# Sparse attention and a feed-forward layer on one core: new planned durations, a new order of loads and a new searched order

## The chip, the cores and the metric

One core of one Trainium2 chip runs the whole program. The metric is device time in microseconds (us); 0.5% of it is 1.2 us.

## What is computed

The reference, cut to what matters: a block-sorted attention, whose output is the input of a two-layer feed-forward part with a leaky rectifier. All inputs and the output are 32-bit floats.

```python
# q, k, v: (4, 8, 768, 64); sort_net: (4, 8, 8, 8); w_in: (512, 2048); w_out: (2048, 512)
P = sort_net
for _ in range(5):
    P = P - max(P, -1); P = exp(P)
    P = P / (sum(P, -1) + 1e-9)
    P = P / (sum(P, -2) + 1e-9)
k_sorted = einsum('bhij,bhjcd->bhicd', P, k_b)     # k, v in 8 blocks of 96 rows
v_sorted = einsum('bhij,bhjcd->bhicd', P, v_b)
scores = q_b @ k_sb.T / 8                          # block by block: 96 x 96
attn = softmax(scores)
x = (attn @ v_sb) as (3072, 512)
h = x @ w_in
g = maximum(h, 0) + alpha * minimum(h, 0)
out = g @ w_out
```

## The kernel before

**Units.** There are 4 batches of 8 blocks, 32 in all, called by number (block 8 is the first of batch 1). A block is 96 tokens with all 8 heads.

**Start (batch 0).** GpSimd issues the loads of q, k (two halves) and v (two halves), line 425 to 452, which convert to 16 bits on their way; the weights follow on the same queue (w_in in 8 pieces, L910, w_out in 2, L915), then k, q and v of batch 1 (KS, QN, VST). Meanwhile VectorE (DVE) and ScalarE (ACT) normalise the 8x8 sorting matrices in five rounds (`sinkhorn`, L518 to 543, result Pb), spread them over the partitions (L552 to 572, result BDK), and TensorE turns q (`prep_q`, L620), sorts and turns k (`prep_k`, L620, 6 units) and sorts v (`prep_v`, L688, 8 units). Before `prep_v`, v is laid out anew (`conv_v`, L677, 4 copies, each on GpSimd or DVE as the planner has it). Results go from PSUM to SBUF by copies on ACT or DVE (L402: QTz, KT, VS).

**Attention (`attention`, L709 on).** For a block: scores (L734), their maximum (L740, DVE). In batch 0 TensorE then computes the scores again with the maximum subtracted (L755, L746), ACT takes the exponential (L778, Es), the output matmul follows (L789), DVE divides (L796, L799, xq), TensorE turns xq (L814) and ACT or DVE copies it into xT. From block 8 on ("far") ACT takes eight exponentials (L767, Esb), a DMA transpose turns them (L772, ET<-Esb), the output matmul follows, and a second DMA transpose (L807) turns xq into xT. The transposes of q for batches 1 to 3 are on the same SP queue (L440, QTz<-QN), as are the output stores (L889).

**Feed-forward part.** `ffn1` (L836): xT by w_in, four matmuls for one of 16 feature tiles over 192 tokens (the first two chunks) or 384; ACT (L846) and DVE (L849) make the rectifier and write hT. Two PSUM banks (psH) take turns, and psYP helps in the first chunk. `ffn2` (L875): hT by w_out, 16 matmuls for 128 tokens in four parts, a copy to outstg (L402), a store (L889).

**What sets the order.** Everything is handed to a planner written into the kernel (`_Graph`). `add` records an operation with its engines, its reads and writes, a planned duration and a priority. `schedule` plays the operations through at build time: each engine takes, of those that are ready by its plan, the one with the lowest priority number, and `span` says when an operation frees its engine and when its result is there. So planned durations decide in which order each engine's instructions stand, and nothing else; on the chip each engine runs its list and waits on semaphores. The string ORDER holds a small number for each operation that is added to its priority; it comes from a search over orders. `span` has rules of its own for DMAs (from GpSimd `loads[0]`, from SP `loads[1]`), for a change of TensorE's tile shape (TILE_NS, `tiles`), and for TensorE's instruction fetch (FETCH, FETCH_NS: a fetch after each 256 instructions, not before 6000 ns after the last one until 58000 ns, 2500 ns after that). Loads of batch 3 wait for the transposes of certain blocks (`paced`).

**Fillers.** `fill` looks for gaps in TensorE's plan ahead of the first output matmul, the first `ffn1` and the first `ffn2`, and puts matmuls without use there (`warm`, L1012, 512 columns), as many as fit into 0.9 of the gap, at 430 ns each up to 6000 ns and 216 ns after.

Of the kernel before, what the change touches and what calls it, by code (L numbers as in the profile page):

```python
# [7 lines left out]
AP = bass.AP  # L8
# [26 lines left out]
FETCH = 256  # L35
FETCH_NS = 6000
FETCH0 = (70, -9000.0, 193)
ORDER = (
    "_o_y1piW010D0f8Q00pym3wBRMstCzMKKZTSWWPAYr3BQscQfaFSqtbihE2YztS9gxhSp8uPJt__IJUtnWBvhzp4dnkehSpmNaJ1Da4EURIcaIMJmV6YT2W0"
    "R2zacnQ3rYyOxuyrG0TzHEr76U6LPQ0G0bPVrYEg70s9y-GwRFyxgyubTIwFhnEwgk4UL2xqZL003Y1QOiPa4msA7MKM3WNS4qSW00UqVFW1prXPpn5Z2d00"  # L40
    "2K2R1g000k6q8e00oz004XHo00ACBuEiAm003zSQv2vFVW7zEcGDW6e-VtiC00T60000F526294EBR9-94Bn00BkDP2_iI7thc34B15Y72ux009rNJitN07q"
    "9iBK3g2JFy4014UDEw6Jvg2VSo3v007UXO0_05Pj0NCMKe3j9gMM3752bt0dvpOd33VpQT3N2l4N5l4YMY5-3o0B0K1YGQD5IC0U3d1K00W-000v1G08001F"
    "6w00S22I5X0pD-0I00Iy3900EkIzrP3QB_0J3qahMuFS3g004E5K002qF00b1a00cRht323q00tauA9DjK8r3Ssp4B132gPe5hWp6b3GFV5i2X0K2x2a565H"
    "1h6bh22C1pAU11gEId2S6S7T002DOzMWE3XiDhjgFZ681W00003223WZ1H1h0s3p5NSD2a0Ate00Jx1g319V0KpQ0t00Je1254303v1K3V007Z00gj1o891h"
    "1Cvr6d1r8rFiDVKxyhQu00CwFcYY8_DSVT9_Ky-ms7160G1v1QJi2sM6II8AEJHC6BH3G43l2A00ou1W4u6ElGGo00Cs01L4LdZp864tJfV900002TKe6fut"
    "7sHlLs1x2u6rNs4m001Y5-8krxRv19ZxZC002zb61uBIKYpBQgWGDPb8Dx00WfB60W40001PYE3z0024A1FY0-aS009m008r0js0Zxzkvuly5i0F00p9lx23"
    "0006AMNu3t00v4qj0xbV0yKwPM00q4-dNpviC2WDGj0U01580000CG6r5H000hSJ1WpN0300SkZF00f2Ha6909AOx95xds-61Ydk8uBPBojGApGCCCHbaN1T"
    "B9dS1P2C2C00QXg300GrBY0yPO0P0N7m4UxxP-FGtd3xeMXAWFQ-00al4hPS3j1k1lIY006ifn00NXPT1h752Y000000000KnHm_kD40Cr0z7n005eI8b5WO"
    "Jv1ZZbUw006B000hqBAT0000790A0023003A7R00000l0q3AWvDUWWsTgd4eyPVNtseSiZCmQgH3F-8O00qkFU00002e0O1M00Vd0Aqa4T-400Y44xEF00Dj"
    "5lth00D1iwFqNUcW9giS9C00O-Q3ck9xCPGAFnCEAQE21JDG7g2B00BE00MNv9oX1RK3Cd00fuE9H7k_bNGW3U7G0HCv00DF04006b7G0Y3g00003rEB000R"  # L50
    "590X00Hc6l8SDF9J5S009P5Shx00EEG00h3r003p6TCB004s1N007UFr009-ex005UOUxI4nGfF7SD5N007w110k2c3700790I00R73L002m0000U20000L5"
    "6T00Ey5W41MVeiML116aF1UbodhgGbq7f-5tJX3K6A8z02b3KF0r4GBZ1nGH3x0000BT2041Op4lBbCvBG0M01BcF100Ad78QO132V0BB-2100004Z07GT0e"
    "0n2h0P0Ud88V0S000y0S00003k0FAi00iI0PiTGL0Q1q0m00ms1a0000Bq005R7J2MCaCb00EW040061N41a1Y2A8P9I3F6FR55o3v001c9LLt1GepUi05Hj"
    "KE2d6m45XL29EvkvNn4AauGk002_411W6Q9m004N-6CH0m00004IUk00BG98Np00EmEA6d1Pki-U00Hg9G0Q2-E_4sKVBU0NCEVaQe0SkaChNC008k3O0000"
    "162tB36S009q7x1lEo140W1N27005rWW9B525tS4cl1YWd2i0Gb_6q4K170f5dBPSf1sh5001hMZiP01bhJDGv5-EXBdFX2PWh0K5r1BTs00FzCk69wsAg00"
    "0w3S00H-d200g9977681KDCRpB00Ot1t0L1z0000xM9E009Q2I00FyJhiT4D7MQgCk1f1GO40000000WlU1H14JLbP003yZL1B8e1D08uh3v00qdhy1F0I00"
    "0Pb-Vt2vluPj0HD12B4R2yC23-5G5U4m00Ne3EOI6x0n943N2j22002eAlA4005830006MAJ00DJ4s00O39F094K4_0R9VEM21091r00StK5004kFS1xaIL_"
    "00pyc53O2a001sZAhh000O0000ZCWk1v0B0z000P000Y000000Fqb-"
# [35 lines left out]
class _Graph:  # L94
# [67 lines left out]
    def schedule(self):  # L162
# [17 lines left out]
        loads = [0.0, 0.0, 0, *FETCH0]  # L180
# [5 lines left out]
        while done < len(ops):  # L186
# [9 lines left out]
            at, e, op = best  # L196
# [23 lines left out]
    def fill(self, make, spans):  # L220

        out, last = [], 0.0
        for op in self.order["pe"]:
            for lo, hi, deps, bank in spans:
                begin = max([last, lo] + [self.ops[d].end + 300 for d in deps])
                unit = 430 if begin < 6000 else 216
                m = int((op.start - begin) * 0.9 / unit)
                if op.start <= hi and m > 0:
                    x = _Op("pe", lambda e, m=m, bank=bank: make(e, m, bank), 0, 0.0, None, len(self.ops))
                    x.start, x.end = begin, begin + m * unit  # L230
                    x.deps.update(deps)
                    self.ops.append(x)
                    out.append(x)
# [77 lines left out]
def bass_sinkhorn_attn__then__act_prelu_kernel(  # L311
# [92 lines left out]
    def t_either(n, mode=1):  # L404
# [3 lines left out]
    G.add(SYNC, lambda e: e.dma_start(P32[:, :], AP(sort_net.tensor, 0, [[64, 32], [1, 64]])), 1990,  # L408
          w=["P"], prio=-100, dma=(dma_sem("sn"), 0))
    G.add(SYNC, lambda e: e.dma_start(alphaR[:, :], AP(moe_alpha.tensor, 0, [[128, 16], [1, 128]])),  # L410
          300, w=["alphaR"], prio=-99, dma=(dma_sem("al"), 0))
# [14 lines left out]
    def load_q(b, prio):  # L426
# [4 lines left out]
        for h in range(H):  # L431
# [4 lines left out]
                dma=(d_qn[h], 2000 * (b == 3)))  # L436

    def turn_q(b, t, prio):
# [6 lines left out]
            prio=prio, dma=(d_qt[t], 0))  # L445

    def load_kv(t, src, name, sem, g, b, prio):
        n = (2, 1, 1, 4)[b]
        for x in range(n):
# [4 lines left out]
                prio=prio + x / 100, dma=(sem[b + x + (b > 0)], 700 * (b == 3 and name == "KS")))  # L454
# [66 lines left out]
    def sinkhorn():  # L521
        pr = -85

        def dv(fn, r, w):
            G.add(DVE, fn, 210, r=r, w=w, prio=pr)
# [100 lines left out]
    def prep_q(u, prio, bank):  # L626
        t, off, row, keys = bank
        G.add(PE, pairs(KZ, 0, u, identb, 0, 128, bank, 6144), 372, r=[("QS", 0), "identb"], w=keys, prio=prio, tiles=(1, 1), mms=16)
# [4 lines left out]
    def conv_k(b, u, prio):  # L633
        n = b % 2
        for hp in range(2):
            o = AP(KZ, hp * 64 * 6144 + 16 * u * 128 + hp * 64, [[6144, 64], [128, 16], [1, 64]])
            i = AP(KS[n], hp * 64 * 3072 + 16 * u * 64, [[3072, 64], [64, 16], [1, 64]])
            G.add(POOL, lambda e, o=o, i=i: copy(e, o, i), 1600,
                  r=[("KS", n, x) for x in range(4)] + [("KZ0", hp)], w=[("KZ", u, hp)], prio=prio)

    def prep_k(b, u, prio, bank=BANK_P):
# [11 lines left out]
        else:  # L653
            G.add(PE, pairs(KS[n], n, u, BDK, b * 128, 512, bank), 372, r=[("KS", n, x) for x in ((u // 3,) if b == 0 else range(4))] + [("BDK", b)], w=keys,
                  prio=prio, tiles=(1, 1), mms=16)
# [9 lines left out]
    def conv_v(b, c, prio):  # L665
        keys = [("VD", 2 * c), ("VD", 2 * c + 1)]
        if b > 1:
            for th in range(2):
                oz = AP(VD32, th * 64 * 4096 + 8 * c * 128 + th * 64, [[4096, 64], [128, 8], [1, 48]])
                iz = AP(VST32[b % 2], th * 64 * 1536 + 8 * c, [[1536, 64], [1, 8], [32, 48]])  # L670
                G.add(POOL, lambda e, oz=oz, iz=iz: e.tensor_copy(oz, iz), 900,  # L671
# [5 lines left out]
        G.add(("dve", "pool"), lambda e: e.tensor_copy(o, i), {"dve": 560, "pool": 1000},  # L677
              r=[("VST", b % 2, x) for x in range(4)], w=keys + [("VDh", 2 * c), ("VDh", 2 * c + 1)], prio=prio)

    def prep_v(b, u, prio, bank=BANK_P):  # L680
# [21 lines left out]
        else:  # L702
            G.add(PE, f, 374, r=[("VD", u), ("VDh", u), "VD0", ("BDK", b)], w=keys, prio=prio, tiles=(1, 1), mms=16)
# [9 lines left out]
    def attention(g, prio):  # L713
# [49 lines left out]
        if far:  # L763
            def ex(e):
# [9 lines left out]
                5000 if g < 18 else 3100, r=[("Esb", me)], w=[("ET", me), ("turned", g)], prio=prio, dma=(d_e[me], 0))  # L774
# [31 lines left out]
        if far:  # L806
            G.add(SYNC, lambda e: e.dma_start_transpose(o2, AP(xq[me], 0, [[512, 96], [1, 512]])),  # L807
                  4400 if g < 18 else 2600, r=[("xq", me)], w=[("xT", g % 16), ("turnx", g)], prio=prio, dma=(d_x[me], 0))
# [49 lines left out]
    def ffn2(t, prios):  # L858
# [11 lines left out]
        for x, (bank, key) in enumerate(banks):  # L870
            for part in range(4):
# [11 lines left out]
                if len(ffn_ops) == 1:  # L883
# [8 lines left out]
                  dma=(d_o[ob + x], 0))  # L892
# [115 lines left out]
    def warm(e, m, bank):  # L1008
        t, off, row, keys = bank
        inst = None  # L1010
        for _ in range(m):
# [45 lines left out]
```

## Time and profile before

| | us |
|---|---|
| time, median of three runs | 244.02 |
| lowest and highest | 243.72, 244.91 |
| the profiled execution | 245.91 |
| its span, first to last instruction | 244.2 |

The profile is of one execution, and durations are read from it. Its mean granted TensorE clock is 0.972 of full speed. In the rows, PE is TensorE's matmuls and PEld its weight loads, which overlap; L numbers are lines of the kernel before (an operation of the kernel after has a line three lower from L402 on). Matmul ends are modelled, so starts are the safer reading.

### The profile page before, as it was taken

To read this page: it belongs to the slowest core of one execution; us is meant where nothing else is said; L and a number is where in the kernel's file an instruction comes from. 1 tells how busy PE (TensorE), PEld (TensorE's weight loads), DVE (VectorE), ACT (ScalarE), POOL (GpSimd) and SP (SyncE) were. 2 spreads that over 40 slices of the span, in tenths; PEclk is the share of its full clock that TensorE was granted. 3 is DMA by queue.
4 is the path that set the end of the run, shared out by engine and by line. 5 is a ranking of instruction groups with operands and counts; after the bars stand their busy time and mean duration, and the time that the engine had idled before them with its cause. 6 is when DMAs were issued, how large, how long until landed. Compare 5 with 4: busy or idle time off the path is not lost.

```text
span 244.2 us, 6048 instructions
## 1 busy us (share of the span) xinstructions
PE 229.2 (94%) x2454; PEld 135.1 (55%) x2454; DVE 168.0 (69%) x341; ACT 151.8 (62%) x419; POOL 75.2 (31%) x97
## 2 busy tenths in 40 slices
PE   4677999999999999999969999999999999999995
PEld 1346667777545655555535565654455555555544
DVE  5877597786868988676736577965769856744540
ACT  5443366777978887675628678764675585454431
POOL 8959930216898000144972900000000000000000
PEclk9996599999999999999979999999999999999999
DMA  5999999999499767699999633432543343011103
GB/s 93 205 194 210 209 198 210 184 211 160 80 173 175 98 102 118 125 111 180 155 169 92 143 66 93 98 93 55 141 97 67 64 136 94 16 44 43 46 0 129
DMA packets 66940, 29.78 MB, mean 122 GB/s; under 512 B 58704, under 2 KB 61536, under 8 KB 66912
## 3 DMA queue, kind: packets, MB, share of 16 engines
q0 software_dynamic: 24256, 13.63, 43.3%
q1 hardware_dynamic: 42656, 15.76, 33.9%
q8 instruction: 19, 0.31, 0.5%
q14 instruction: 9, 0.07, 0.1%
HBM read 27.28 MB, written 6.29 MB: 137 GB/s over the span
## 4 chain that ended last, share of the span: by engine, by line
PE 80%; DMA 12%; DVE 4%; ACT 2%; POOL 1%; issue 1%; POOLq 0%
PE psH L836 32%; PE psYP L875 26%; DMA ET<-Esb 7%; DMA VST<-in_v_dram 5%; PE psS L875 4%; PE psO L789 3%; PE psS L734 3%; PE psYP L696 1%; PE psYP L688 1%; PE psS L746 1%; PE psYP L648 1%; DVE VD L677 1%; PE psYP L620 1%; PE psS L755 1%; PE psH L1012 1%; ACT t L846 1%
## 5 line engine op out<-in xcount | busy, mean ns | idle before, releaser
L849 DVE SCALAR_TENSOR_TENSOR hT<-t,omaT,psH 128x384 bf16<-128x384 f32 (+1 forms) x139 | 77.7, 571 | 42.1 <-ACT t L846 40.1
L836 PE MATMUL psH<-xT,w_in_bf 128*128 128x384 bf16 (+1 forms) x556 | 99.7, 314 | 0.6 <-DVE hT L849 0.4
L846 ACT ACTIVATE t<-psH 128x384 f32<-128x384 f32 (+1 forms) x139 | 62.8, 464 | 47.9 <-PE psH L836 43.6
L875 PE MATMUL psYP<-w_out_bf,hT 128*128 128x512 bf16 x336 | 84.0, 380 | 0.0
L836 PEld LDWEIGHTS psH<-xT,w_in_bf 128*128 128x128 bf16 x556 | 50.1, 98 | 34.8 <-DVE hT L849 4.4
L767 ACT ACTIVATE Esb<-psS,nf 96x96 bf16<-96x96 f32 x192 | 46.2, 343 | 5.0 <-DVE nf L740 4.7
L875 PEld LDWEIGHTS psYP<-w_out_bf,hT 128*128 128x128 bf16 x336 | 30.7, 98 | 28.7 <-DVE outstg L402 0.2
L740 DVE TENSOR_REDUCE nf<-psS 96x8 f32<-96x768 f32 x24 | 22.7, 947 | 5.8 <-PE psS L734 5.5
L799 DVE TENSOR_TENSOR xq<-psO,rec 96x512 bf16<-96x512 f32 x31 | 21.2, 684 | 0.7
L432 POOL DMA_DIRECT2D QN<-in_q_dram x24 | 20.3, 866 | 3.1 <-DMA xT<-xq 1.5
L671 POOL COPY VD<-VST 64x384 int32<-64x384 int32 x16 | 13.6, 847 | 8.1 <-PE psYP L688 7.0
L402 ACT ACTIVATE VS<-psYP 112x512 bf16<-112x512 f32 x19 | 13.0, 685 | 2.6 <-PE psYP L696 1.9
L402 POOL COPY KZ<-KS 64x1024 bf16<-64x1024 bf16 x12 | 12.4, 1036 | 5.5 <-DMA KS<-in_k_dram 4.8
L789 PE MATMUL psO<-VS,ET 112*128 112x65 bf16 x192 | 9.9, 194 | 2.2 <-DMA ET<-Esb 2.1
L789 PEld LDWEIGHTS psO<-VS,ET 112*128 112x128 bf16 x192 | 8.7, 98 | 6.0 <-DMA ET<-Esb 3.1
L466 POOL DMA_DIRECT2D VST<-in_v_dram x6 | 3.3, 546 | 27.2 <-DMA ET<-Esb 23.8
L1012 PE MATMUL psYP<-identb 128*128 128x512 bf16 x26 | 8.2, 453 | 3.4 <-ACT identb L402 3.4
L734 PE MATMUL psS<-KT,QTz 64*128 64x96 bf16 x248 | 11.1, 211 | 0.1
L402 ACT ACTIVATE outstg<-psYP 128x512 f32<-128x512 f32 x12 | 7.2, 597 | 5.9 <-PE psYP L875 5.9
L734 PEld LDWEIGHTS psS<-KT,QTz 64*128 64x128 bf16 x248 | 6.4, 96 | 6.1 <-ACT t L846 3.1
L875 PE MATMUL psS<-w_out_bf,hT 128*128 128x512 bf16 (+1 forms) x48 | 9.6, 344 | 0.0
L796 DVE RECIPROCAL rec<-psO 96x8 f32<-96x8 f32 x31 | 6.2, 200 | 4.7 <-PE psO L789 4.4
(136 smaller groups left out, 200.9 us busy)
## 6 DMA issues: line engine op xcount, KB each, us to landing
out_dram<-outstg SPq DMA_DIRECT2D x23, 256.0 KB, 2.3
QN<-in_q_dram POOLq DMA_DIRECT2D x24, 96.0 KB, 6.7
w_in_bf<-in_moe_w_in_dram POOLq DMA_DIRECT2D x8, 256.0 KB, 16.1
w_out_bf<-in_moe_w_out_dram POOLq DMA_DIRECT2D x2, 1024.0 KB, 26.7
VST<-in_v_dram POOLq DMA_DIRECT2D x4, 384.0 KB, 19.1
KS<-in_k_dram POOLq DMA_DIRECT2D x2, 768.0 KB, 25.0
KZ<-in_q_dram POOLq DMA_DIRECT2D x1, 768.0 KB, 6.7
KS<-in_k_dram POOLq DMA_DIRECT2D x2, 384.0 KB, 9.0
```

The source lines that it names most:

```text
L402: return e.activation(o, i, ACTF.Copy) if e is nc.scalar else e.tensor_copy(o, i)
L432: G.add(POOL, lambda e, h=h: e.dma_start(AP(QN, h % 4 * 128 + (h // 4) * 64, [[3072, 128], [512, 6], [1, 64]]), AP(q.tensor, b * HB + h * ...
L671: G.add(POOL, lambda e, oz=oz, iz=iz: e.tensor_copy(oz, iz), 900, r=[("VST", b % 2, 2 * th + x) for x in range(2)] + ["VDz"] * th, w=[("VD ...
L734: inst = e.matmul(o, AP(QTz[n], hp * 64 * QP + h4 * 768 + i * 96, [[QP, 64], [1, 128]]), AP(KT[n], hp * 64 * ld + (h4 * 8 + i) * bk, [[ld, ...
L740: G.add(DVE, lambda e: e.tensor_reduce(AP(nx, 0, [[8, 96], [4, 2], [1, 4]]), AP(psX, 0, [[1024, 96], [512, 2], [96, 4], [1, 96]]), AxisLis ...
L767: inst = e.activation(AP(Esb[me], p * 128, [[1024, 96], [64, 2], [1, 48]]), AP(psX, (p // 4) * 512 + (p % 4) * 96, [[1024, 96], [48, 2], [ ...
L789: inst = e.matmul(AP(psZ, hp * 512 + h4 * 68, [[1024, 128], [1, 65]]), AP(ET[me] if far else Es0[m], pos(h4, hp) * 96, [[800, nk], [1, 128]]),
L799: G.add(DVE, lambda e: e.tensor_tensor(out=AP(xq[me], 0, [[512, 96], [256, 2], [64, 4], [1, 64]]), in0=AP(psZ, 0, [[1024, 96], [512, 2], [ ...
L836: inst = e.matmul(AP(pt, poff, [[1024, 128], [1, n]]), AP(w_in_bf, kt * DFF + ft * 128, [[KT_TILES * DFF, 128], [1, 128]]), AP(xT, kt * XR ...
L846: G.add(ACT, lambda e: e.activation(AP(t1[tb], 0, [[T1W, 128], [1, n]]), AP(pt, poff, [[1024, 128], [1, n]]), ACTF.Relu, scale=-1.0), t_ac ...
L849: G.add(DVE, lambda e: e.scalar_tensor_tensor(out=AP(hT, ft * RING + tok % RING, [[FT_TILES * RING, 128], [1, n]]), in0=AP(t1[tb], 0, [[T1 ...
L875: inst = e.matmul(AP(bank[0], bank[1], [[1024, 128], [1, n]]), AP(hT, ft * RING + tok % RING, [[FT_TILES * RING, 128], [1, 128]]), AP(w_ou ...
```

## The change

All edits but the ORDER string change planned durations or rules of the planner, or the fillers. The string ORDER is another one throughout, and with it the order on every engine. In the list of instructions GpSimd's loads of batch 0 stand as v, v, q, k, k (before: q, k, v, k, v), with w_in six times, w_out, w_in twice behind (before: w_in eight times, then w_out); of the four copies of `conv_v` for batch 0 one stands on GpSimd between the w_in issues, two on DVE between rounds four and five of the normalising, and one on DVE behind BDK (before: one on GpSimd and three on DVE, all behind the k copies). Fillers are 32 of 512 columns and 21 of 128 (before: 31 of 512).

```diff
-FETCH = 256
-FETCH_NS = 6000
-FETCH0 = (70, -9000.0, 193)
 ORDER = ( ... another string ... )
@@ span
                 loads[2] = op.tiles[1]
-                loads[3] += 2 * op.mms
-                if loads[3] > loads[5]:
-                    loads[5] += FETCH
-                    late = loads[4] + (FETCH_NS if at < 58000 else 2500) - at
-                    if late > 0:
-                        d += late
-                    loads[4] = at + (late if late > 0 else 0)
             return at + d, at + d
         if e == "pool":
-            begin = max(loads[0], at + 1400)
-            loads[0] = begin + op.dur
-            return at + 780, begin + op.dur + (2500 + op.dma[1])
-        if op.dur < 2000:
+            begin = max(loads[0], at + 1400 + 400 * (at > 40000))
+            loads[0] = begin + op.dur * (1.2 if loads[1] > begin else 1)
+            return at + 780, loads[0] + (2500 + op.dma[1])
+        if not op.dma[1]:
             return at + 1200, at + op.dur
-        loads[1] = max(max(at, loads[0]) + op.dur, loads[1] + 1000)
-        return at + 1300, loads[1]
+        loads[0] = max(at + 500, loads[0]) + op.dma[1]
+        loads[1] = max(loads[0], loads[1] + 780)
+        return at + 1300, loads[1] + 1200
@@ fill
-                unit = 430 if begin < 6000 else 216
-                m = int((op.start - begin) * 0.9 / unit)
+                if begin < 6000:
+                    m, s = int((op.start - begin) / 430), 0
+                    dur = m * 430
+                else:
+                    m = max(0, int((op.start - begin) * 0.95 / 216))
+                    s = max(0, int(((op.start - begin) * 0.95 - m * 216) / 56))
+                    dur = m * 216 + s * 56
@@ planned durations (ns), and the second number of dma=(semaphore, ns)
 sort_net load          1990 -> 2400
 alpha load             300 -> 1700
 q load of batch 3      dma 2000 -> 0
 turn_q                 dma 0 -> 900
 load_kv                dma 700 for k of batch 3 -> 700 for the second half of v of batch 0
 sinkhorn, last step    210 -> 430
 prep_q                 372, tiles (1, 1) -> 255, tiles (0, 1)
 conv_k                 1600 -> 1050
 prep_k, batches 0, 1   372, tiles (1, 1) -> 255 (batch 0) or 375, tiles (0, 1)
 conv_v, batches 2, 3   900 -> 860
 conv_v, batches 0, 1   dve 560, pool 1000 -> dve 530, pool 870
 prep_v, batches 0, 1   tiles (1, 1) -> (0, 1)
 transpose ET<-Esb      5000 if g < 18 else 3100, dma 0 -> 3100, dma 1400
 transpose xT<-xq       4400 if g < 18 else 2600, dma 0 -> 2600, dma 950
 output store           dma 0 -> 600
@@ warm
-        for _ in range(m):
-            inst = e.matmul(AP(t, off, [[row, 128], [1, 512]]), identb[:, :], AP(identb, 0, [[128, 128], [0, 4], [1, 128]]))
+        for n in [4] * m + [1] * s:
+            inst = e.matmul(AP(t, off, [[row, 128], [1, 128 * n]]), identb[:, :], AP(identb, 0, [[128, 128], [0, n], [1, 128]]))
```

More of the change, by code (lines that the diff above doesn't have):

```diff
@@ L225, in fill @@
                 begin = max([last, lo] + [self.ops[d].end + 300 for d in deps])
-                unit = 430 if begin < 6000 else 216
-                m = int((op.start - begin) * 0.9 / unit)
-                if op.start <= hi and m > 0:
-                    x = _Op("pe", lambda e, m=m, bank=bank: make(e, m, bank), 0, 0.0, None, len(self.ops))
-                    x.start, x.end = begin, begin + m * unit
+                if begin < 6000:
[5 more added lines that the diff above has]
+                    dur = m * 216 + s * 56
+                if op.start <= hi and m + s > 0:
+                    x = _Op("pe", lambda e, m=m, s=s, bank=bank: make(e, m, s, bank), 0, 0.0, None, len(self.ops))
+                    x.start, x.end = begin, begin + dur
+                    x.mms = 0
                     x.deps.update(deps)
```

76 lines of the change are left out of this document (38 added, 38 removed).

## Prediction

> **What bounds the kernel now.** The page comes first, with the share of each engine.
>
> ```profile
> span 244.2 us, 6048 instructions
> ...
> PE 229.2 (94%) x2454; PEld 135.1 (55%) x2454; DVE 168.0 (69%) x341; ACT 151.8 (62%) x419; POOL 75.2 (31%) x97
> ```
>
> TensorE is busy for 94% of the span, no other engine for 70%. A table by stage shows where TensorE has spare time, and where it was granted less than its full clock.
>
> ```profile
> 18.00:30.00 12.00, 10.24 (x181) 7.46 (x181) 8.22 (x14) 4.50 (x7) 11.79 (x14) 0.58 1.17 209
> ...
> 31.50:60.00 28.50, 28.30 (x508) 21.02 (x507) 22.58 (x56) 20.64 (x47) 7.00 (x10) 1.00 1.39 189
> ...
> 120.00:130.00 10.00, 7.86 (x54) 4.07 (x53) 4.82 (x9) 4.56 (x15) 7.42 (x10) 0.83 1.30 146
> ```
>
> Columns: stretch, its length, busy PE, PEld, DVE, ACT, POOL, then the clock (0.58 in the first row). So there are three parts. Up to 31.5 us, the start of the feed-forward part (FFN), TensorE waits for data. From there it is full, and only its own work counts. In 120 to 130 it loses 2.1 us idle and 17% of the clock, some 1.7 us, so 3.8 us. The timeline of TensorE and the chain that ended last tell what was late there:
>
> ```profile
> 125.23 0.42 PE L789 MATMUL psO<-VS,ET 112*128 112x65 bf16 x8 [2.14 <-DMA ET<-Esb]
> ```
>
> ```profile
> 117.15 8.03 DMA ET<-Esb
> ```
>
> The output matmul of a block waited for the DMA transpose of its probabilities, which took 8.03 us. The same chain, for the start:
>
> ```profile
> 3.94 12.65 DMA VST<-in_v_dram
> 16.61 2.71 DVE VD L677 x3
> ...
> 21.85 0.96 DVE nm L740
> ...
> 24.90 0.43 PE psS L755 x8
> 25.33 0.75 PE psS L746 x8
> ```
>
> ```profile
> 27.60 0.65 PE L789 MATMUL psO<-VS,Es 112*128 112x65 bf16 x8
> ...
> 31.54 0.26 PE L836 MATMUL psH<-xT,w_in_bf 128*128 128x192 bf16 x1
> ```
>
> The second half of v is the last of the first loads, and lands at 3.94 + 12.65 = 16.59. From there to the first FFN matmul it is 14.95 us: three conversions of v one after the other, the copies of VS, then the scores, maximum, exponential and output of blocks 1 and 0. From the output matmul of block 0 (27.60) to the FFN it is 3.94 us.
>
> **The work of TensorE** is the same in both: the order of instructions has the same count of every shape, but for the fillers, 31 of 512 columns before, 32 of 512 and 21 of 128 after. What moves is when the FFN starts and what TensorE waits for afterwards.
>
> **Start: a new order of loads.** Before it is q, k, v, k, v; the new order has v, v, q, k, k. The bytes of the five are equal, so the last lands at about 16.6 again, but it is k. Durations that the steps below use, by group, from the timeline, from the view of the tile VST and from the DMA issues:
>
> ```profile
> L778 ACT ACTIVATE Es<-psS 112x768 bf16<-112x768 f32 x7 | 5.7, 810 | 3.4 <-PE psS L746 3.1
> L402 DVE CAST KT<-psYP 128x512 bf16<-128x512 f32 x8 | 5.5, 688 | 0.6 <-PE psYP L620 0.4 <-PE psYP L648 0.2
> ```
>
> ```profile
> 13.65 0.29 DVE L572 TENSOR_TENSOR BDK<-mkh,dsel 128x128 bf16<-128x128 f32 x1
> ```
>
> ```profile
> L677 DVE COPY VD<-VST x5: 492/496/1215, 16.6 to 50.2; 128x384 int32<-128x384 int32 x5
> ```
>
> ```profile
> KZ<-in_q_dram POOLq DMA_DIRECT2D x1, 768.0 KB, 6.7
> ```
>
> The first load (q, as many bytes as all of v) lands 6.7 us after its issue, so v will be there at about 8. Its four conversions now stand one on GpSimd, two between the normalising steps on DVE, one behind BDK: the 2.71 us leave the path. Their price is a later Pb. Two conversions at 0.49 us, each in a wait of about 0.3 for ACT's exponential, and three reductions moved in among the first steps make it some 0.5 us later (an estimate: 2 x 0.2 over the wait, and what of the reductions the waits don't hold); q, now landing near 12, puts a copy of 0.69 ahead of BDK, which ends near 15.1 instead of 13.9 (13.65 + 0.29). The three k units of the first half then still run before the second half lands at 16.6, which is the cover: past a slip of another us, each us is one on the path.
>
> From k on: two of the three last k units on TensorE to 17.2 (0.3 each, taken from the scores' 0.27 below), two DVE copies of 0.69 behind each other to 18.6, the scores at 18.7. DVE then holds a VS copy, a maximum (0.95), a VS copy and block 0's maximum: 19.3 + 0.95 + 0.69 + 0.95 = 21.9. Two groups of matmuls in the durations above (0.43 and 0.75) end at 23.3, the exponential (0.81) at 24.1. Ahead of block 0's output stand the fillers, three of 512 and two of 128. Their price has two ends; the trace has fillers at the full clock (the second row):
>
> ```profile
> 3.42 3.69 PE L1012 MATMUL psYP<-identb 128*128 128x512 bf16 x10 [3.42 <-ACT identb L402]
> ...
> 9.71 1.47 PE L1012 MATMUL psYP<-identb 128*128 128x512 bf16 x6
> ```
>
> Six in 1.47 are 0.25 each, and at 0.58 of the clock 0.42. So the fillers take 0.8 to 1.5 us behind block 1's output (23.3 to 23.8), and block 0's starts at 24.6 to 25.3. With the 3.94 us from there to the FFN, it starts at 28.5 to 29.2; at full clock in place of 0.58 the 1.18 of the two groups would be 0.7 and the start 28.0. I take **28.6, a gain of 2.9**. The bounds are 3.5 and, if Pb slips by the 1.2 us that BDK does, 2.0 on top of the cold end.
>
> Here the clock decides. In 18 to 30 us it was 0.58 although TensorE's longest wait up to 31.5 us, but for that for the first filler, was 1.7 (the waits of this stretch, in us: total, count, longest):
>
> ```profile
> PE psYP L552 <- DVE Pb L543: 1.7, 1, 1.7
> ```
>
> The Trainium skill (TensorE: Matmul & The Clock Gate, section "HAM oscillation — how this bites in real kernels") gives as its rule that no idle gap over about 3.4 us may occur. By it TensorE would have stayed warm here and will after the change, and the FFN would start at 28.0. The trace disagrees: gaps of at most 1.7 us went with 0.58. So warmth isn't counted on. The new order also leaves some 2 us empty ahead of q: its 19 fillers are planned at 0.43 each, and ten took 3.69, later ones 0.25, so they end near 3.8 + 3.7 + 2.2 = 9.7, and q lands near 12.
>
> **Old and new planned durations.** The old planner held the probabilities' transpose (L772) at 5.0 us up to block 17; the new one at 3.1 plus what the DMA queue holds. What it was:
>
> ```profile
> DMA to landing us min/median/max: 2.9/4.1/6.0
> ```
>
> ```profile
> DMA to landing us min/median/max: 5.3/6.7/8.3
> ```
>
> The first row is 60 to 104 us, the second 104 to 126. So blocks are packed closer. I priced each row of both orders with the trace's own steps:
>
> ```profile
> 138.34 1.30 PE psH L836 x8
> 139.64 0.86 PE psYP L875 x4
> ```
>
> (0.65 for a group of four at 384 columns, 0.86 for the second layer's four, 0.27 for scores, whose 0.34 below overlaps the next group, and the like), and added what lies between scores and output of each block. For blocks 8 to 15 it was 8.3, 10.1, 9.2, 7.6, 9.9, 8.5, 12.4, 10.7 us; it is 7.2, 7.0, 8.4, 7.4, 6.1, 8.0, 7.3, 7.9. What must fit in:
>
> ```profile
> 60.87 0.34 PE L734 MATMUL psS<-KT,QTz 64*128 64x96 bf16 x8
> ...
> 64.23 1.21 SPq L772 DMA_TRANSPOSE ET<-Esb  x1
> ...
> 69.95 0.41 PE L789 MATMUL psO<-VS,ET 112*128 112x65 bf16 x8
> ```
>
> Scores to issue is 3.36 us, so with the landing 6.3 (at 2.9), 7.5 (at 4.1), 9.4 (at 6.0). The span from 60.87 to 69.95 is 9.08 where the sum with the scores' own 0.27 gives 8.57, so sums run at 1.06. The eight become 7.9, 7.7, 9.2, 8.1, 6.8, 8.8, 8.0, 8.7: at 7.5 only block 12 waits, 0.7; at 2.9 nobody. **I take 1.5 us of new waits**, ends 0 and 5.7 (below). For blocks 16 to 19, where the 8 us transposes fell, the distance was 11.8, 12.4, 9.0, 8.1 and is 9.2, 9.4, 12.5, 10.3: the block that waited 2.14 us (18) has 3.5 us more room. So I take its 3.8 us as gone. Next late would be 16: 10.0 against 3.4 + 6.7.
>
> The other new costs (sinkhorn, conversions, the DMAs' queue) only feed the planner. Fillers inside the FFN grow by 0.3 us.
>
> **Sum**, against the profiled execution: 245.91 (span 244.2 and 1.7 around it) - 2.9 - 3.8 + 1.5 + 0.3 = 241.0, a change of -4.9. That execution lies 1.9 over the median of 244.02. If the excess is part of the 3.8, the median comes to 241.0, if not, to 239.1. I take the middle, **240.1**, by itself 238.0 to 242.6: 1.5 less waits and 0.4 on the start below, 0.9 on the start and 1.6 of waits above.
>
> **Rivals.**
> 1. *Waits among blocks 8 to 15 eat the gain.* With 6.0 us for each transpose (the maximum above) waits are 1.5 for block 8, 0.2, 0, 1.3, 1.3, 0, 1.4, 0, as a wait also gives room to the block behind: 5.7. A wait of 5.0 in place of 1.5 gives 243.6. For it: the distances. Against: the median of 4.1.
> 2. *Slower: the transposes stay slow past 104 us as well.* 5.7 as above; at 8.3 blocks 16 and 19 wait 1.7 and 0.5; one such wait cools the clock as at 125, 1.7. That is 9.6, and 245.91 - 2.9 - 3.8 + 9.6 + 0.3 = 249.1, +3.2 or 247.2 on the median. It decides from a mean landing of about 6 us over blocks 8 to 17. Against: 4.1, and room of 12.5 at block 18.
> 3. *Instruction fetch.* The old planner let TensorE take 256 instructions in 6 us up to 58 us; the new one has dropped this.
>
> ```profile
> q8 instruction: 19, 0.31, 0.5%
> ```
>
> ```profile
> 13.00:19.00 6.00, 4.87 (x168) 3.30 (x167) 4.42 (x8) 3.06 (x6) 3.27 (x6) 1.00 1.10 194
> ```
>
> 19 fetches of 16 KB for 4908 matmuls and weight loads are 256 each. The new start puts some 470 matmuls, 940 with their loads, ahead of the FFN, 3.7 times 256. At 6 us for each that is 22 us from about 10 us on, so the FFN would begin at 31.5 or later: no gain there, 240.1 + 2.9 = 243.0. Against: 335 ran in the 6 us from 13.
>
> That the closer fillers don't keep the clock up, so that the change doesn't do what it says, lies in the 28.6 (29.2 by itself).
>
> **Chances.** Forecast 0.60, rival 1 0.15, rival 3 0.11, rival 2 0.14. Faster or slower begins at 0.5% (1.2 us), about what a measurement of this kernel tells from no change. Faster: 0.60, and 0.05 each of rivals 1 and 3, 0.70. Same: 0.10 and 0.06, 0.16. Slower: 0.14. The range 237.5 to 245.0 leaves out 0.06 below and 0.14 above.
>
> **What would show it.** Right: the first L833 at 28.0 to 29.2; k, not v, the last load of the chain; no wait over 1 us for ET at 120 to 130, clock 1.0 there; small waits for ET between 60 and 104. Wrong: an FFN start past 30.5 with waits put down to "issue" (rival 3), or ET waits of over 4 us in all (1 and 2), or a clock below 0.9 past 32 us.

## The result, and the profile after

The kernel after takes **253.61 us** (median of four, 252.83 to 254.63), the kernel before on the same chip 243.87 (241.21 to 244.91): a ratio of **1.044**, with a 95% interval of 1.034 to 1.054. It is slower, where the forecast was 240.1. The profiled execution took 254.12 (span 252.4). Ratios, here and below, leave out disturbed executions, so one can differ from that of the medians beside it.

The waits of TensorE in the kernel after (total, count, longest):

```profile
PE psO L786 <- DMA ET<-Esb: 6.3, 4, 4.2
...
PE psS L731 <- issue: 3.3, 1, 3.3
...
PE psO L685 <- issue: 0.7, 1, 0.7
```

The table by stage (columns as before: busy PE, PEld, DVE, ACT, POOL, clock, DMA share, GB/s):

```profile
18.00:30.00 12.00, 8.38 (x194) 6.23 (x194) 4.80 (x8) 5.49 (x8) 11.83 (x14) 0.79 1.17 208
...
60.00:104.00 44.00, 40.87 (x499) 24.01 (x492) 35.36 (x64) 31.97 (x95) 15.76 (x18) 1.00 0.81 110
104.00:126.00 22.00, 17.77 (x131) 8.96 (x129) 12.93 (x22) 11.29 (x37) 8.80 (x13) 0.88 1.13 124
```

And the places, from the timeline of TensorE and the chain that ended last:

```profile
18.32 0.19 PE L685 MATMUL psO<-BDK,VD 128*64 128x64 bf16 x1 [0.73 <-issue]
...
24.62 0.21 PE L731 MATMUL psS<-KT,QTz 64*128 64x96 bf16 x1 [3.30 <-issue]
...
33.89 0.34 PE L833 MATMUL psH<-xT,w_in_bf 128*128 128x192 bf16 x2
...
121.75 0.62 PE L786 MATMUL psO<-VS,ET 112*128 112x65 bf16 x8 [4.23 <-DMA ET<-Esb]
```

```profile
111.91 9.80 DMA ET<-Esb
```

Two things are to be seen. In the start TensorE stands for 3.30 us between the seventh and the eighth matmul of one group of eight, with nothing to wait for that the profile shows, and the FFN starts at 33.89 instead of 28.6. In the body the transpose of block 16 takes 9.80 us and TensorE waits 4.23 for it, with the clock at 0.88 over 22 us. That mean covers the wait itself; from the end of the wait to 126 us the clock was 0.50, and 0.83 from there to 130, which costs an estimated 4.25 x 0.50 + 4 x 0.17 = 2.8 us:

```profile
121.75:126.00 4.25, 4.25 (x24) 1.75 (x25) 1.84 (x3) 0.00 (x0) 3.84 (x6) 0.50 1.30 170
126.00:130.00 4.00, 4.00 (x26) 2.13 (x25) 0.61 (x1) 3.00 (x11) 1.96 (x3) 0.83 1.43 105
```

Against the sum of the forecast (241.0 for the profiled execution, 254.12 measured, so 13.1 missing):

| | forecast | measured | difference |
|---|---|---|---|
| start of the FFN | 28.6 | 33.89 | 5.3 |
| block 16: wait, and clock behind it | 0 | 4.23 + 2.8 | 7.0 |
| other waits for ET | 1.5 | 6.3 - 4.2 | 0.6 |
| together | | | 12.9 |

The remaining 0.2 are not traced. That the start is late is no accident of one execution: in the seven traces whose head is that of the kernel after, unchanged, the FFN starts at 32.7 to 34.9, in the four with the head of before at 28.3 to 31.5.

### The profile page after: what moved, and what is told of

It reads as the page before. It is cut to its first block, busy times and chain, and to the rows that moved or that the text cites. A ratio compares the mean times of both kernels' runs of the same rounds, so it can differ in the third digit from the quotient of the medians.

```text
span 252.4 us, 6069 instructions
## 1 busy us (share of the span) xinstructions
PE 231.7 (92%) x2476; PEld 135.7 (54%) x2476; DVE 169.2 (67%) x345; ACT 149.7 (59%) x414; POOL 76.7 (30%) x98
## 3 DMA queue, kind: packets, MB, share of 16 engines
q1 hardware_dynamic: 42656, 15.76, 32.1%
## 4 chain that ended last, share of the span: by engine, by line
PE 81%; DMA 13%; issue 2%; ACT 1%; DVE 1%; POOL 0%; POOLq 0%
PE psH L833 29%; PE psYP L872 27%; DMA ET<-Esb 9%; DMA KZ<-in_q_dram 4%; PE psO L786 4%; PE psS L872 3%; PE psS L731 3%; PE psYP L693 1%; PE psS L743 1%; PE psYP L685 1%; PE psYP L1009 1%; PE psH L1009 1%; PE psYP L617 1%; PE psO L685 1%; PE psYP L645 1%
## 5 line engine op out<-in xcount | busy, mean ns | idle before, releaser
L833 PE MATMUL psH<-xT,w_in_bf 128*128 128x384 bf16 (+1 forms) x556 | 98.3, 312 | 0.6 <-DVE hT L846 0.6
L872 PE MATMUL psYP<-w_out_bf,hT 128*128 128x512 bf16 x336 | 87.0, 385 | 0.3 <-DVE outstg L399 0.3
L872 PEld LDWEIGHTS psYP<-w_out_bf,hT 128*128 128x128 bf16 x336 | 30.7, 99 | 28.6 <-issue 1.1
L1009 PE MATMUL psYP<-identb 128*128 128x512 bf16 (+1 forms) x41 | 10.3, 386 | 3.9 <-ACT identb L399 3.9
L399 ACT ACTIVATE VS<-psYP 112x512 bf16<-112x512 f32 x15 | 10.3, 685 | 4.9 <-PE psYP L693 2.7
L399 DVE CAST KT<-psYP 128x512 bf16<-128x512 f32 x12 | 8.3, 689 | 4.4 <-PE psYP L645 2.9
```

Of the source, the lines that this page charges most:

```text
L399: return e.activation(o, i, ACTF.Copy) if e is nc.scalar else e.tensor_copy(o, i)
L833: inst = e.matmul(AP(pt, poff, [[1024, 128], [1, n]]), AP(w_in_bf, kt * DFF + ft * 128, [[KT_TILES * DFF, 128], [1, 128]]), AP(xT, kt * XR ...
L872: inst = e.matmul(AP(bank[0], bank[1], [[1024, 128], [1, n]]), AP(hT, ft * RING + tok % RING, [[FT_TILES * RING, 128], [1, 128]]), AP(w_ou ...
L1009: inst = e.matmul(AP(t, off, [[row, 128], [1, 128 * n]]), identb[:, :], AP(identb, 0, [[128, 128], [0, n], [1, 128]]))
```

## Experiments

**The theories.** 1: TensorE runs out of instructions; a block of 256 (128 matmuls with their loads) comes late while the loads run. 2: in the body the new order brings block 16's transpose among the loads of batch 3, with less room than before. Rivals: the order of the loads or a cold clock makes the start late; the body is late only because the start is; packing alone makes the waits.

Except in the repetition, the kernels do not plan: the order of the planner is written out as a list, which gives each engine the same instructions as the kernel it was taken from, and then edited. Line numbers are those of the kernel after, fillers excepted (L1007). "Head" is what a kernel plans ahead of its first FFN matmul, "body" the rest.

```diff
-    total = G.plan(ORDER)
...
-    G.fill(warm, ...)
+    follow(PLAN)
```

| run | us, median | before, same chip | ratio, 95% |
|---|---|---|---|
| few fillers | 251.85 | 245.99 | 1.024 (1.015 to 1.033) |
| before, fillers split | 248.11 | 245.99 | 1.010 (1.001 to 1.019) |
| head before, body after | 248.09 | 245.99 | 1.016 (1.009 to 1.023) |
| head after, body before | 245.64 | 245.99 | 1.002 (0.997 to 1.007) |
| after again | 253.33 | 245.73 | 1.040 (1.031 to 1.048) |
| after, no loads of batch 3 | 245.77 | 245.73 | 1.008 (1.004 to 1.013) |
| after, outputs later | 254.79 | 245.73 | 1.043 (1.031 to 1.054) |
| q first, body before | 246.62 | 245.73 | 1.013 (1.005 to 1.020) |
| before, no loads of batch 3 | 242.18 | 244.82 | 0.997 (0.991 to 1.002) |
| before, outputs 18 and 19 later | 242.04 | 244.82 | 0.996 (0.991 to 1.001) |
| after, weights late | 260.58 (one) | 244.82 | |
| weights behind the fetch | 252.57 | 244.22 | 1.039 (1.034 to 1.044) |
| after, copies first | 252.26 | 245.32 | 1.028 (1.023 to 1.033) |
| after, outputs later, copies first | 248.11 | 245.32 | 1.014 (1.009 to 1.019) |

### The start: fewer and more instructions

```diff
 few fillers (kernel after)
-    32 of 512 columns, 21 of 128, in 14 groups
+    19 of 512 columns, the first group
```

> The kernel after with its first group of 19 fillers only; the 34 later ones (13 of 512 columns, 21 of 128) are left out, and nothing else moves. Theory 1 (instruction fetch): a block of 256 TensorE instructions (128 matmuls with their weight loads) arrives some 6 us behind the one ahead of it while the loads run. Without 11 fillers (22 instructions) ahead of the first stop and some 12 more ahead of the second, the stops come that much later in the work: the wait of 3.30 for 'issue' leaves line 731 and stands in the second scores or the output matmuls of blocks 1 and 0 (lines 752, 743, 786), and is smaller, 1 to 3 us; the third boundary is no longer ahead of the FFN. The FFN starts at 30.5 to 32.0 in place of 33.9, and the time is 250 to 252. Rival (the late start comes from the order of the loads or from the cold clock, which fillers hold up): the stop stays in line 731 or the FFN starts at 33.9 or later, time 253.6 or more.

```diff
 fillers split (kernel before): first five groups
-    10, 6, 4, 3, 1 of 512 columns
+    40, 24, 16, 12, 4 of 128 columns
```

> The kernel before; the first four groups of fillers (10, 6, 4 and 3 of 512 columns), the fifth as well (1 of 512), are written as four times as many of 128 columns: the same columns for TensorE, 72 more matmuls, 144 more instructions. Theory 1 (instruction fetch): the boundaries of 256 come 144 instructions earlier in the work, there are waits for 'issue' of 2 us and more in all ahead of the FFN that the kernel before has not, the FFN starts at 33.5 to 37 in place of 31.5, and the time is 246 to 249.5. Rival (no limit by instructions; the old rule of 256 in 6 us described nothing): the FFN starts at 31.3 to 31.8 and the time stays 243.9 within 0.5%.

With few fillers the FFN starts at 31.72, as theory 1 said, and the stop is 1.69 and elsewhere, though in line 685 and not in the second scores, where it was expected. The time falls less than that, since the clock is at 0.89 from 30 to 60 us. With split fillers theory 1's 33.5 to 37 was **wrong**: the FFN starts at 31.8, which is what the rival expected, and there is one stop of 1.20. (The time, 248.11, is not the rival's; there is a wait for ET of 3.1 us further on.) The added instructions run while TensorE waits for data anyway, so it also enters each block earlier (its 223rd matmul starts at 14.8, in the kernel before at 17.3), and the next one is asked for earlier.

Where the stops fall is the better evidence. The windows from the first instruction to the middle of the stop, in four kernels (after, few fillers, q first, fillers split):

```profile
0.00:24.50 24.50, 14.91 (x350) 9.04 (x350) 15.91 (x64) 11.34 (x25) 21.68 (x36) 1.00 0.97 175
```

```profile
0.00:24.60 24.60, 16.19 (x350) 10.60 (x350) 17.85 (x65) 11.55 (x25) 21.22 (x36) 0.86 0.96 174
```

```profile
0.00:23.90 23.90, 14.46 (x350) 9.39 (x350) 17.01 (x65) 11.17 (x25) 20.44 (x36) 0.93 0.95 173
```

```profile
0.00:21.15 21.15, 13.09 (x350) 11.91 (x350) 15.33 (x61) 10.12 (x24) 17.37 (x31) 1.00 0.93 169
```

Always 350 matmuls and 350 weight loads, in four different places of the program and at times from 21.15 to 24.6. Between the two stops of the kernel after there are 128 matmuls (here the columns are length, busy PE, clock, DMA share, GB/s):

```profile
18.30:24.60 6.30, 3.00 (x128) 1.00 1.14 206
```

So the stops belong to the count of instructions, not to the work.

### The start: the loads taken away from the fetch

```diff
 after, weights late: 20 loads (w_in, w_out, batch 1) on GpSimd
-    issued from 4.5 to 22 us
+    each waits for the second scores of blocks 0 and 1 (L743)
```

> The kernel after; the loads of w_in, w_out and batch 1 (20 issues on GpSimd) are issued only once the second scores of blocks 0 and 1 are done, so that no load is under way from the landing of k (15.9 us) until then. Nothing else moves; the FFN then waits for its weights, which costs several us behind this point and isn't looked at. Theory 1b (TensorE's next 256 instructions are slow to come because they queue with the loads): they come in 3 us or less in place of 5 to 6, the waits for 'issue' ahead of the second scores (0.7 and 3.3) fall to 0.8 at most in all, the last second scores (line 743, psS) start at 24 to 25.2 in place of 27.5. Rival (a fixed rate of 256 in 6 us, whatever the loads do): waits for 'issue' of 3 us or more again.

Its timeline on TensorE:

```profile
20.27 0.59 PE L731 MATMUL psS<-KT,QTz 64*128 64x96 bf16 x8
...
22.61 0.52 PE L743 MATMUL psS<-identb,nm 96*128 96x96 bf16 x8
...
24.03 0.42 PE L786 MATMUL psO<-VS,Es 112*128 112x65 bf16 x8
...
35.48 0.80 PE L833 MATMUL psH<-xT,w_in_bf 128*128 128x192 bf16 x4 [8.19 <-DMA w_in_bf<-in_moe_w_in_dram]
```

Both stops are gone; the scores of line 731 run as one group of eight, the last second scores start at 22.61 (24 to 25.2 expected), and TensorE is ready for the FFN at 35.48 - 8.19 = **27.29**. The clock is 1.00 from 18 to 30. So of the 6.6 us from 27.29 to the 33.89 of the kernel after, 4.0 are the two stops (0.73 and 3.30); the other 2.6 go with the clock, 0.63 behind the second stop. Whether the stop made the clock low is not shown: the kernel before had 0.58 there without a stop. The traffic shows why the stops are gone. Both windows hold one fetch; this is the kernel with late weights from 17.5 to 19.3, which passes the count of its first stop at 17.6, and the kernel after from 22.1 to 23.2 (share of 16 engines at the end of each row):

```profile
DMA packets 1, 0.02 MB, mean 9 GB/s; under 512 B 0, under 2 KB 0, under 8 KB 0
...
q8 instruction: 1, 0.02, 3.0%
```

```profile
q0 software_dynamic: 132, 0.21, 104.8%
q8 instruction: 1, 0.02, 5.4%
```

Alone, the fetch is done by 19.2, 1.6 us behind the count that asks for it. In the kernel after it is asked for at 18.3, when the first stop ends, and is there only by 23.1, 4.8 us later, beside 132 packets of loads; the stop ends at 24.6. The packet itself takes 0.9 us in both (3.0% of 16 engines over 1.8 us, 5.4% over 1.1); what differs is the time until it moves. A fixed rate of 256 in 6 us is excluded: theory 1b holds, by one execution here and by the version further below.

### The start: entering the blocks earlier, and a version that doesn't pay off

```diff
 q first (head of after, body of before)
-    loads v, v, q, k, k; 19 fillers; two copies of v between the normalising rounds
+    loads q, v, v, k, k; 12 fillers; these copies behind BDK
```

> The kernel with the head of after and the body of before, changed in the head alone: q is loaded first, then v, v, k, k; the first group of fillers has 12 in place of 19; the two copies of v that stood between the normalising rounds on VectorE stand behind BDK, the one on GpSimd two issues later. Theory 1 (each block of 256 TensorE instructions comes some 6 us behind the start of the one ahead; with q third TensorE enters the second block only at 13 us, with q first at 9 to 10.5): blocks end at 16, 22 and 28, TensorE gets there later than that, so the wait of 3 us for 'issue' falls below 0.7, the FFN starts at 28.5 to 30.5 in place of 34.2, and the time is 4 to 6 us below that kernel's 245.64. Rival (the stop at this place has nothing to do with when TensorE starts on q): a wait of 2.5 us or more for 'issue' again, FFN at 32.5 or later.

The expectation failed: a stop of 2.55, the FFN at 33.0, both as the rival had them.

```profile
23.97 0.35 PE L685 MATMUL psO<-BDK,VD 128*64 128x64 bf16 x10 [2.55 <-issue]
```

TensorE did enter the second block early (at 9.5), but it then waited 3.1 us for Pb, and entered the next one only at 18.4, with the data of k. So what counts seems to be the last entry ahead of the dense work, not the first; this reading was made after the run, and no further run tests it.

```diff
 weights behind the fetch (head of after; body of before, blocks 18 and 19 as below)
-    w_in, w_out, batch 1 issued from 4.5 us
+    each waits for the first unit of v on TensorE (L685); w_in first, in its order of use
```

> A version put together from the findings: the head of the kernel after (v, v, q, k, k), the body of the kernel before with the outputs of blocks 18 and 19 moved 2.5 us later, and the loads of the weights and of batch 1 issued only once the first unit of v is through TensorE (line 685, near 17.7 us), the eight pieces of w_in first and in the order of their use. Theory 1b (the queue of loads is what makes instructions late): the loads' data flow from about 19.2 us, behind the fetch that follows from 17.5; waits for 'issue' of 0.8 us at most ahead of the FFN. The first four pieces of w_in land by about 26 and the FFN starts at 27.3 to 29, its ninth feature tile waits 0 to 2 us for the other four; with theory 2d for the body the time is 238.5 to 241.5, 3 to 6 us below the kernel before. Rival (what the loads lose while they are held back is missing later: w_out, k, q and v of batch 1 come some 4 us later): FFN at 27.3 to 29, but waits for w_in, w_out or QTz of 3 us or more, time 242 to 246.

```profile
PE psYP L872 <- DMA w_out_bf<-in_moe_w_out_dram: 6.0, 1, 6.0
```

The first half came true: no stop over 0.8, the FFN at 27.8, six us earlier than in the kernel after. The rival named the rest, larger than it was priced: what the queue lost while the loads were held back is missing behind, TensorE wants w_out at 32.1 and has it at 38.1, a wait of 6.0, and the time is 252.57. The wait is not all: behind it the clock was 0.52 up to 44 us (an estimated 5.9 x 0.48 = 2.8 us), and from 60 to 104 TensorE is busy for 39.70 of 44 us, in the run with the same body behind the head of before for 42.27.

### The body: halves exchanged

```diff
+    operations ahead of the FFN by the planned start in one kernel, in its order; all others in the order of the other
```

> All operations that the kernel before plans ahead of its first FFN matmul, in its order with its fillers; all others in the order of the kernel after. Theory 2 (the two losses are independent, and most of it is in the body: the order from the FFN on costs 5.9 us by itself): FFN at 31.5, a wait for ET of 3 to 5 us near 120, time 249.5 to 251.5. Rival (the body is slow only because the late start shifts its transposes into the loads of batch 3): no wait for ET over 1.5 us near 120, time 244 to 247.

> All operations that the kernel after plans ahead of its first FFN matmul, in its order with its fillers; all others in the order of the kernel before. Theory 2 (independent losses): the start alone, FFN at 33.9 with the wait of 3.3 for 'issue', no wait for ET over 2.5 us, time 245.5 to 247.5. Rival (the late start makes the body late): time 249 or more.

> The kernel after, unchanged, for its own spread. Both theories: 'issue' wait of 3 to 3.6 in line 731, FFN at 33.6 to 34.2. Theory 2a (the wait in block 16 comes of this order, which brings its transpose among the loads of batch 3 every time): a wait for ET of 3 to 5 us near 120 again, ratio to the kernel before 1.03 to 1.05. Rival (chance of one execution): no wait for ET over 2 us near 120, ratio 1.01 to 1.02.

```profile
PE psO L786 <- DMA ET<-Esb: 4.7, 4, 2.5
```

```profile
104.00:126.00 22.00, 21.74 (x167) 11.75 (x170) 16.12 (x28) 14.44 (x48) 12.77 (x18) 1.00 1.36 162
```

The first row is the body of after behind the head of before: 4.7 us of waits, so the body is slow by itself; but its longest wait is 2.5 where 3 to 5 were expected, and its time, 248.09, lies between the ranges of theory 2 and of the rival. The second row is the body of before behind the head of after, full, without a wait for ET, at 245.64: theory 2's range. The two losses don't add: 1.6% and 0.2% against 4.0% for both (the kernel after again, 253.33, where the wait near 120 was there again, 3.8 us).

### The body: the loads, the room, and what stands behind them

```diff
 no loads of batch 3 (kernels after and before)
-    16 loads of k, q, v into KS, QN, VST for batch 3
```

> The kernel after without the 16 loads of k, q and v of batch 3 (everything else stays, so batch 3 is computed from the data of the batch before it in the same buffers). Theory 2a (the DMA transposes of blocks 15 to 19 are slow because these loads share the DMA engines): the transpose of block 16 lands in 3 to 5 us in place of 9.8, the wait of 4.2 near 120 falls below 0.5 and the clock there stays above 0.97, all waits for ET come to 2.5 at most, time 5 to 8 us below the kernel after on this chip. Rival 2b (the blocks stand too close whatever the loads do): waits for ET of 4 us or more in all, time within 3 us of the kernel after.

> The kernel before without the 16 loads of k, q and v of batch 3 (batch 3 is computed from the data of the batch before it in the same buffers). Leaving them out of the kernel after was worth 7.6 us. Theory 2c (the loads cost the new order far more than the old, because block 16 has 9.3 us of TensorE work between scores and output there in place of 11.8, and because the last v load of batch 3 comes 8.5 us later): 1 to 4 us here. Rival (the loads cost both orders the same, and the body's loss is something else): 6 us or more here.

The transposes ET<-Esb from 104 to 126 us, in the kernel after and without the loads:

```profile
DMA to landing us min/median/max: 2.8/7.6/9.8
```

```profile
DMA to landing us min/median/max: 2.8/2.8/2.8
```

Without the loads the kernel after takes 7.6 us less, with waits for ET of 1.4 in all. The kernel before gains about 0.9 us by its ratio (0.997, which can't be told from none; the medians lie 2.6 apart), and at most 2.2 by the interval's end of 0.991. So the loads cost the new order more than three times what they cost the old one. That is what theories 2a and 2c say, though 2c's 1 to 4 us for the kernel before is not shown; its rival, 6 or more, is excluded.

```diff
 outputs later (kernel after)
+    L786, L793, L796, L804 of blocks 8, 9, 10, 12 to 19: planned start + 2500
```

> The kernel after with the output matmul, division and second transpose of blocks 8, 9, 10 and 12 to 19 moved 2.5 us later in the planned order (work of TensorE between scores and output 8.4 to 12.5 us for most of them in place of 6.2 to 9.5; the kernel before has 7.7 to 12.6). Theory 2b (distance): all waits for ET come to 2.5 us at most in place of 6.3, the one near 120 to 2 at most, time 3 to 6 us below the kernel after on this chip. Rival (the landing time in the loads sets the wait, or the room taken comes back as waits of the first layer for xT): time within 2 us of the kernel after.

The waits for ET did go, and the time did not move (254.79), so distance alone (2b) **fell**. What came in place, and why, on GpSimd (second fence):

```profile
PE psYP L693 <- POOL VD L668: 3.6, 1, 3.6
...
PE psH L833 <- DMA xT<-xq: 1.3, 2, 0.8
...
PE psO L786 <- DMA ET<-Esb: 0.6, 1, 0.6
```

```profile
131.87 0.56 POOL L447 DMA_DIRECT2D KS<-in_k_dram  x1 [4.25 <-DMA xT<-xq]
132.41 0.84 POOL L429 DMA_DIRECT2D QN<-in_q_dram  x1
133.29 3.49 POOL L668 COPY VD<-VST 64x384 int32<-64x384 int32 x4
```

The last four copies of v stand behind a load of k that waits 4.25 us for block 16's second transpose (`paced`), itself slow in the same loads. The kernel after has the same three rows at 132.51 to 133.94, hidden behind its wait for ET. In the kernel before these copies stand ahead of that load. Two further runs, to settle it:

```diff
 copies first (kernel after), alone and with the outputs later
-    GpSimd: KS and QN of batch 3 (last of k, one head of q), then four copies L668
+    GpSimd: four copies L668, then these two loads
```

> The kernel after; on GpSimd two loads of batch 3 (the last quarter of k and one head of q) that wait for the second transpose of block 16 stand behind the last four copies of v (line 668) in place of ahead of them. Nothing else moves. Theory 2e (two things are late in the body at once, the transpose of block 16 and behind it these copies, so each alone hides the other): the wait of 3.8 to 4.2 for ET near 120 stays, time within 1.5 us of the kernel after's 253.33. Rival (the copies alone set the body): 2.5 us or more less.

> Both edits: the outputs of blocks 8, 9, 10 and 12 to 19 moved 2.5 us later, and the two loads of batch 3 behind the four copies of v. The fourth load of v landed at 127.6 in the run with the outputs later alone, so the copies can run at 128 to 131.5, ahead of the 135.05 at which line 693 got them. Theory 2e: the wait for VD falls from 3.6 to 0.5 at most, those for ET stay below 1, time 249 to 252 (254.79 with the outputs later alone). Rival (a third wait, for xT, KS or QTz, takes its place): 253.5 or more.

```profile
104.00:126.00 22.00, 18.25 (x120) 9.10 (x120) 12.52 (x22) 11.39 (x37) 7.62 (x12) 0.85 1.23 116
```

```profile
104.00:126.00 22.00, 21.17 (x163) 11.13 (x164) 15.10 (x28) 14.49 (x48) 10.76 (x15) 1.00 1.06 151
```

The copies alone change little: 252.26 against 253.33, with the waits for ET still there (6.9 in all, the longest 3.3; first row). These are runs on two chips, and by their ratios, 1.028 and 1.040, whose intervals just overlap, a gain of 1% is not excluded. Both together give **248.11**, 6.7 below the outputs alone and below the range expected (second row: TensorE 21.17 of 22, clock 1.00), though a wait of 1.2 for VD remained where 0.5 was expected. So of the 7.6 us that the loads cost the kernel after, some 5.2 (253.33 - 248.11, on two chips) were two waits in one place, each of which hid the other.

```diff
 before, outputs of blocks 18 and 19 later
+    L786, L793, L796, L804 of blocks 18, 19: planned start + 2500
```

> The kernel before with the output matmul, division and second transpose of blocks 18 and 19 alone moved 2.5 us later in the planned order (TensorE's work between scores and output 11.8 and 10.8 us in place of 9.1 and 8.2); no load waits for these two. Theory 2d (a wait for ET of about 2 us in block 18 and the low clock behind it is what the kernel before loses at 120 to 130): no wait for ET over 0.5 us there, clock above 0.97 from 104 us on, time 1.5 to 3.5 us below the kernel before. Rival (the room comes back as waits of the first layer for xT, or the wait is in few executions only): within 1 us of it.

The wait in block 18 of the kernel before is gone (0.2 us for ET in all) and the clock is at 1.00. The median is 2.8 lower, but the ratio of 0.996 (0.991 to 1.001) doesn't exclude no change. By its median it is the fastest version here; that it beats the kernel before isn't shown.

## Why the prediction was wrong

**The start, up to 21 us, was right in its times, not in its path.** The conversions of v left the path, and the first scores came at 19.7 (forecast 18.7), block 0's at 21.0. But the last load of the chain that ended last was q, not k:

```profile
2.54 9.35 DMA KZ<-in_q_dram
```

It landed at 11.89, TensorE waited 1.79 for it, and from there to the first stop the chain is TensorE's own work. (Of the two conversions between the normalising rounds one stands behind round three and one behind round four, at 9.17 and 11.01.) With instructions at hand the rest holds too: ready at 27.29 and starting at 27.84 in the two runs that cleared the fetch, against the forecast 28.6, and 28.0 at full clock.

**The step that failed first is the start's gain of 2.9**, which put the instruction fetch at nothing. The fetch was rival 3, with a chance of 0.11. Its mechanism, its sign ("waits put down to issue", FFN past 30.5) and its bound of 31.5 or later were on the page; FFN at 33.89 fits them. It was set aside by one sentence, "Against: 335 ran in the 6 us from 13". That row counts across a boundary whose block was already there. Counted from one boundary to the next, the kernel before was itself close to the limit: the 128 matmuls up to its second boundary end near 22.9, having begun near 17.2, and in two runs with its head TensorE stopped there for 0.7 us. The fetch for the block that begins there was done at 21.57, 1.5 us ahead. Before the change those 256 instructions took 5.7 us for want of data (v came last); the new order has data for 256 in 2.8 (17.6 to 20.4 in the run with late weights). The term of 2.9 us gained was a 2.4 us loss, 5.3 off. The 6 us of the old planner are thus the price beside the loads: from stop to stop it is 6.3 us (18.32 to 24.62), 4.8 for the fetch and 1.5 until TensorE goes on.

**The second step that failed is "next late would be 16: 10.0 against 3.4 + 6.7".** 6.7 is a median over a stage. Block 16's own transpose, among the loads in both kernels, took 8.3 in the kernel before (the maximum quoted) and 9.8 after. With it the sum is 11.7 to 13.2 against 10.0. In the trace, scores to issue were 4.1 (107.79 to 111.91) and TensorE was there 9.7 us behind the scores: 4.1 + 9.8 - 9.7 = 4.2, the wait. Rival 2 had these numbers and priced block 16 at 1.7, but with a chance of 0.14; its time of 247.2 was short of the truth because the start was wrong as well.

**The third is "the other new costs only feed the planner".** The new durations moved GpSimd's list: copies of v behind a load that waits for a transpose. That wait wasn't in the sum. It didn't add to the time by itself; it is what kept the time when the first wait was removed.

**Waits among blocks 8 to 15** (1.5 forecast, 2.1 measured) were right, as was the equal work of TensorE. All three signs that the prediction gave for being wrong came: the FFN past 30.5 with a wait for "issue", over 4 us of waits for ET, and a clock below 0.9 past 32 us. Two slips in its sum are small: 21.9 with the groups of 0.43 and 0.75 ends at 23.1, not 23.3, and the 0.4 on the start below is 0.6 (3.5 - 2.9).

**Why the halves exchanged don't add up** (1.6% and 0.2% against 4.0%) can be read in part from the profiled executions. The kernel before has a loss of its own, the 3.8 us in block 18, and neither exchanged kernel has it. With the head of after the FFN starts 2.7 us later (34.24) and the 3.8 are gone: 2.7 - 3.8 = -1.1, measured 244.66 - 245.91 = -1.3. With the body of after there are 4.7 us of waits for ET and some 1.7 of clock (0.51 from 117.5 to 121 us) in place of the 3.8: 2.6, measured 247.97 - 245.91 = 2.1. So the loss that goes is counted in both differences. These sums are of one execution each; for the medians the question stays open.

## What to carry to other kernels

A rule in a planner that looks arbitrary may be the price of a real resource: count TensorE's instructions between boundaries, from the last wait for data to the first dense stage, not over any six microseconds. Work out a late transfer with the row of that very transfer, not a median of its stage, and ask what is second in line there: where one wait goes and the time stays, the waits of the new trace name the next. Loads held back to clear a path are missing later.

## What the runs showed of the hardware

- TensorE's instructions come in blocks of 256 (128 matmuls and as many weight loads from stop to stop), and the times of the fetches fit a next block asked for when one is entered. The fetch was done 1.6 and 1.9 us later with nothing else on the DMA engines (the run with late weights, blocks entered at 17.60 and 20.66) and 3.9, 4.8 and 5.1 us later with the loads (the kernel after, blocks entered at 13.12, 18.32 and 24.62); behind a stop TensorE went on 1.3 to 1.5 us after its end (17.06 to 18.32 and 23.13 to 24.62 in the kernel after).
- The same head had another clock in each execution. Four runs with the head of before, from 18 to 30 us: 0.58, 0.72, 0.86, 1.00, and the FFN at 31.5, 31.3, 30.3, 28.3. The last, from the run of the kernel before without batch 3's loads, which changes nothing ahead of 98 us:

```profile
18.00:30.00 12.00, 10.09 (x233) 7.24 (x234) 10.56 (x23) 6.43 (x12) 11.79 (x14) 1.00 1.16 208
```

- After the stop of 3.30 us the clock was 0.63 for the next 9.3 us (first row), and after the stop of 2.55 us in the run with q first it was 0.62 for 9.0 (second row). By the rule weighed in the prediction (the Trainium skill, TensorE: Matmul & The Clock Gate, "HAM oscillation — how this bites in real kernels", no gaps over about 3.4 us) it would have stayed warm. 3.30 is too near to that bound to tell; with 2.55 the trace disagrees again:

```profile
24.60:33.87 9.27, 9.25 (x118) 0.63 1.17 216
```

```profile
23.97:33.00 9.03, 9.03 (x111) 0.62 1.18 213
```
